# Three later scans of a linear-attention kernel: both decay factors from one VectorE product, their signed copies from ScalarE, and the cap on the inverse length moved

## The chip, the cores and the metric

The kernel runs on one core of one Trainium2 chip. The metric is the device time of one execution in microseconds (us). A core has TensorE (PE, with its weight loads shown as PEld), VectorE (DVE), ScalarE (ACT), GpSimd (POOL) and SyncE (SP), which issues the DMAs here.

## The reference, cut to what matters

Four batches, eight heads, 768 tokens, 48 features a head. A complex decay, clipped in length, drives a linear attention; what comes out goes through a Fourier mixer with an MLP, then a token MLP and a second channel MLP.

```python
mag = np.sqrt(a_re * a_re + a_im * a_im)
scale = np.minimum(mag, 0.999) / (mag + 1e-06)
ar, ai = a_re * scale, a_im * scale            # the normalized factor
for t in range(S):
    S_re, S_im = ar*S_re - ai*S_im + k v, ar*S_im + ai*S_re
    y[t] = q[t] @ S_re
x -> x + real(fft(fft(x))) -> norm -> MLP -> token MLP -> MLP
```

## The kernel before, in words

Each batch has a **chain** (the functions `scan`, the chunk part of `stage1`, and `stage2`, the mixer) and a **dense** part (`mlp`, `tok1`, `tok2`, `mlp2`). The dense part of batch b-1 is emitted beside the chain of batch b. The chain of batch 0 has a scan of its own (`first_scan`), which this change touches only in where its small tile `both` is allocated; `scan` runs for batches 1, 2 and 3 and is called the first, second and third later scan here.

A later scan holds 64 chunk halves on two sets of 64 partitions and walks through 49 steps of cumulative products. Sixteen tiles have three steps each and the seventeenth has one. For each tile `st_b` to `st_d` compute the length of the decay; `st_e` makes the factor tile `A`; `st_f` does the steps on VectorE in PSUM (L623, L624, L625); `st_g` multiplies queries and keys by the running product (L634, L635, L637); `st_t` transposes them on TensorE (L650).

`A` has five planes of 48 features a step: plane 0 the real factor, plane 1 its copy, plane 2 the squared inverse factor, plane 4 the imaginary factor times a per-partition sign `sgn` (-1 on the lower 64 partitions, +1 on the upper), plane 3 the negative of plane 4. The common scaling is `c1` (written by VectorE, L595). Plane 0 is a GpSimd product (L597), plane 4 a VectorE product with the sign (L599), planes 1, 2 and 3 come from ScalarE (L598, L600, L601). Plane 2 drives a third running product, the squared inverse length. At the second step of each tile (`j == CL`, CL is 1) VectorE takes the minimum of that product and `R_CAP` in place (L620); there are 48 of these in the three scans.

In program order the factors of tile i+1 are made after step two of tile i (`part2(i + 1)` in the loop at the end of `scan`). `A` has two buffers; `raw`, the loaded decays, share a tag of ten buffers (`"e"`).

The order on each engine's queue is found at build time by a scheduler that goes by priorities and a time estimate of its own; on VectorE, ScalarE and GpSimd the dense stream comes first, then the weight conversions, then the chain; on TensorE the chain comes first. Engines execute their queues in that order. During the first later scan the kernel also converts 64-bit-packed weights into two-part fp32 weights (`convert`: ScalarE L191, L192, L205; VectorE L194, L199; GpSimd L196, L206; a DMA in, L185, and one out, L207).

Of the kernel before, what the change touches and what calls it, by code (L numbers as in the profile page):

```python
# [8 lines left out]
F32 = mybir.dt.float32  # L9
# [3 lines left out]
ACTF = mybir.ActivationFunctionType  # L13
ALU = mybir.AluOpType
# [9 lines left out]
NT = 3  # L24
# [5 lines left out]
CF = (2, 2, 2, 2, 2, 0, 8, 0)  # L30
AN = (5, 6, 6, None)
WC = (0, 0, 0, 0, 0, 0, 10, 12)
WZ, CL = 0, 1
XL = (0,), (0, 1, 2, 3, 4, 5)
AH = 4
KS, EN = 5, 3
# [1 line left out]
XP = [((0, 96), (96, 96), (192, 96), (288, 96))] + [((0, 288), (288, 96))] * 4  # L38
NR = [((0, 192),)] * 5
KT, PF, PD = (0, 1), ((2, 0), (2, 1)), (((1, 0), (1, 1)), ((1, 1),))  # L40
O = (0, 1, 0)
HOLD = mybir.DependencyInfo(mybir.DependencyClass.NoSync, mybir.DependencyReason.SCHED_ONLY)
CHK_A, CHK_E = 6.0e4, 1.0e-7
CHK_B, CHK_C, R_CAP = 1.5e-9, 1.0e18, 1.0e24
# [4 lines left out]
def with_ap(ap, offset, dims):  # L49
    return bass.AP(ap.tensor, ap.offset + offset, [list(ap.ap[0])] + [list(d) for d in dims])  # L50
# [3 lines left out]
def attn_fft_mixer_kernel(ctx: ExitStack, tc: tile.TileContext, aL, xL, vL, wL, qN, kN, vN, arN, aiN,  # L54
# [37 lines left out]
    def alloc(tag, shape, dt=F32, name=None):  # L92
        n = 1
        for x in shape[1:]:
            n *= x
        t = pool.tile([128, SIZE[tag]], dt, tag=tag, bufs=BUFS[tag], name=name or tag)
        return shaped(t[0:shape[0], 0:n], shape)
# [21 lines left out]
    sgn = misc[:, 224:225]  # L119
# [14 lines left out]
        ge.memset(gm[j], 0.0)  # L134
    xT = pool.tile([112, 4, S], F32, name="xT")
    chk = pool.tile([128, 3], F32, name="chk")
    low = pool.tile([128, len(SL4)], F32, name="low")
    lnc = pool.tile([128, 5], F32, name="lnc")
    tiny, shift, top, eps, wee = (lnc[:, j:j + 1] for j in range(5))
# [174 lines left out]
    def first_scan(t, knd, qk):  # L314
# [7 lines left out]
        big = {}  # L322
        last = [None]
        away = []
        both = pool.tile([128, 2], F32, name="both")

        def vq(x):

# [219 lines left out]
    def scan(b, t, knd, qk):  # L548
# [40 lines left out]
        def st_e(i):  # L589
            d = t[i]  # L590
            n, raw, tm = d["n"], d["raw"], d["tm"]
            x, r, tt, c1 = (tm[:, j, :].rearrange("p (a c) -> p a c", c=48) for j in range(4))
            A = alloc("A", [128, 4, 240], name="A")
            A = with_ap(A, 0, [(240, n), (48, 5), (1, 48)])
            ve.scalar_tensor_tensor(out=c1, in0=r, scalar=-2.0 / ACL, in1=tt, op0=ALU.max, op1=ALU.mult)  # L595
            ve.scalar_tensor_tensor(out=x, in0=r, scalar=-2.0 / ACL, in1=x, op0=ALU.min, op1=ALU.mult)
            ge.tensor_tensor(out=A[:, :, 0, :], in0=raw[:, :, 0, :], in1=c1, op=ALU.mult)  # L597
            se.copy(out=A[:, :, 1, :], in_=A[:, :, 0, :])  # L598
            (ge if O[2] else ve).scalar_tensor_tensor(out=A[:, :, 4, :], in0=raw[:, :, 1, :], scalar=sgn, in1=c1, op0=ALU.mult, op1=ALU.mult)  # L599
            se.activation(out=A[:, :, 2, :], in_=x, func=ACTF.Square)  # L600
            se.activation(out=A[:, :, 3, :], in_=A[:, :, 4, :], func=ACTF.Copy, scale=-1.0)  # L601
            d["A"] = A
            P = palloc("p", [128, NT, 144])
            d["P"] = P[:, 0:n, :].rearrange("p n (c f) -> p n c f", c=3)

        def st_f(i, j):
            d = t[i]
            P, A = d["P"], d["A"]
            s = d["s0"] + j
            if s == 0:  # L610
                se.copy(out=P[64:128, 0, 0, :], in_=A[64:128, 0, 0, :])
                se.copy(out=P[64:128, 0, 1, :], in_=A[64:128, 0, 4, :])
                se.copy(out=P[64:128, 0, 2, :], in_=A[64:128, 0, 2, :])
                ve.memset(P[0:64, 0, 0, :], 1.0)
                ve.memset(P[0:64, 0, 1, :], 0.0)
                ve.memset(P[0:64, 0, 2, :], 1.0)
                return
            prev = P[:, j - 1] if j else t[i - 1]["P"][:, t[i - 1]["n"] - 1]
            if j == CL:
                ve.tensor_scalar(out=prev[:, 2, :], in0=prev[:, 2, :], scalar1=R_CAP, scalar2=None, op0=ALU.min)  # L620
            cur = P[:, j]
            y = ytmp[s % 2]
            ve.tensor_tensor(out=cur, in0=prev, in1=A[:, j, 0:3, :], op=ALU.mult)  # L623
            ve.tensor_tensor(out=y, in0=prev[:, 1::-1, :], in1=A[:, j, 3:5, :], op=ALU.mult)  # L624
            ve.tensor_tensor(out=cur[:, 0:2, :], in0=cur[:, 0:2, :], in1=y, op=ALU.add)  # L625

        def st_g(i):
            d = t[i]
            m, P, xx, s0 = d["m"], d["P"], d["xx"], d["s0"]
            y1, y2 = ybuf[0][i % 2], ybuf[1][i % 2]  # L630
            x1 = xx[:, :, 0, :].unsqueeze(2).to_broadcast([128, m, 2, 48])
            o1 = with_ap(y1, 0, [(128, m), (64, 2), (1, 48)])
            o2 = with_ap(y2, 0, [(128, m), (64, 2), (1, 48)])
            ve.tensor_tensor(out=o1, in0=x1, in1=P[:, 0:m, 0:2, :], op=ALU.mult)  # L634
            ve.tensor_tensor(out=xx[:, :, 1, :], in0=xx[:, :, 1, :], in1=P[:, 0:m, 2, :], op=ALU.mult)  # L635
            x2 = xx[:, :, 1, :].unsqueeze(2).to_broadcast([128, m, 2, 48])
            ve.tensor_tensor(out=o2, in0=x2, in1=P[:, 0:m, 0:2, :], op=ALU.mult)  # L637
            sp.dma_start(out=knd[0, :, s0:s0 + m, :], in_=y1[0:64, 0:m, :])
            sp.dma_start(out=knd[1, :, s0:s0 + m, :], in_=y2[64:128, 0:m, :])
# [721 lines left out]
```

## Time and profile before

| | |
|---|---|
| median of 3 runs | 1092.18 us (1091.67 to 1096.09) |
| profiled execution: its time / its span | 1093.5 us / 1091.7 us |
| TensorE busy | 978.8 us (90%) |
| VectorE busy | 769.3 us (70%) |
| ScalarE busy | 511.1 us (47%) |
| GpSimd busy | 417.9 us (38%) |
| mean granted TensorE clock | 0.966 |

The span runs from the first to the last instruction. Busy time merges overlapping instructions of one engine. An instruction's duration includes its pipeline's fill and drain, so neighbours on VectorE or ScalarE can overlap a little. The share of an engine over the whole span is an average over stages with different limits.

### The profile page before, as it was taken

The page shows a single profiled execution, that of the slowest core. Times are in us where ns is not written, and L with a number is a line of the kernel's source. Part 1 is how long each engine was busy: PE and PEld are TensorE (multiplying, and loading weights), DVE is VectorE, ACT ScalarE, POOL GpSimd, SP SyncE. Part 2 cuts the span into 40 slices and gives each one's busy share as a digit, 9 for nine tenths or more (in the row PEclk, how much of TensorE's full clock was granted, in tenths as well). Part 3 has the DMA queues.
Part 4 walks back from the last instruction along what each step waited for, and adds up shares of the span by engine and source line. Part 5 has one row for each costly group of instructions (what it writes and reads, how often), then busy time and mean ns, then how long its engine had stood idle before and what let it go on. Part 6 is the DMA issues. An engine that isn't in the chain of part 4 may idle for free.

```text
span 1091.7 us, 21067 instructions
## 1 busy us (share of the span) xinstructions
PE 978.8 (90%) x7314; PEld 915.3 (84%) x7314; DVE 769.3 (70%) x2083; ACT 511.1 (47%) x1425; POOL 417.9 (38%) x541
## 2 busy tenths in 40 slices
PE   1567788999899988999998999999897999999997
PEld 0337766989788986899997899999787999999997
DVE  6988887999999678999658879974734433433332
ACT  6753446777875236877216556842224112121111
POOL 6625994673676454345336312424512002000000
PEclk9988896999999999899999999999998999999999
DMA  6238943776668563465575345665303434543432
GB/s 219 48 101 233 290 165 118 252 264 206 200 235 270 162 180 113 117 184 175 156 198 148 100 139 187 203 165 132 128 17 117 146 114 135 159 156 127 163 101 76
DMA packets 101537, 174.66 MB, mean 160 GB/s; under 512 B 11056, under 2 KB 61104, under 8 KB 100912
## 3 DMA queue, kind: packets, MB, share of 16 engines
q1 hardware_dynamic: 101424, 173.24, 51.5%
q8 instruction: 60, 0.98, 0.4%
q14 instruction: 53, 0.43, 0.1%
HBM read 133.88 MB, written 39.32 MB: 159 GB/s over the span
## 4 chain that ended last, share of the span: by engine, by line
PE 68%; DVE 16%; DMA 6%; POOL 4%; ACT 3%; issue 2%; SPq 0%; POOLq 0%; DVEq 0%; ACTq 0%
PE l L956 24%; PE l L934 23%; PE s L761 4%; DMA cvt<-wL 3%; PE s L650 2%; PE s L1047 2%; PE s L810 2%; DVE cvt L199 2%; DVE ws L1002 2%; PE s L1036 1%; PE s L816 1%; PE s L1161 1%; POOL cvt L196 1%; DVE ws L996 1%; PE s L1179 1%
## 5 line engine op out<-in xcount | busy, mean ns | idle before, releaser
L956 PE MATMUL l<-w,h 128*128 128x384 f32 x1728 | 326.5, 339 | 6.8 <-DVE h L947 4.0
L934 PE MATMUL l<-th,w 128*128 128x384 f32 x1152 | 316.0, 344 | 8.8 <-DVE h L947 4.3
L956 PEld LDWEIGHTS l<-w,h 128*128 128x128 f32 x1728 | 297.2, 188 | 11.1 <-DVE h L947 6.3
L934 PEld LDWEIGHTS l<-th,w 128*128 128x128 f32 x1152 | 213.1, 191 | 12.2 <-DVE h L947 6.1
L934 PE MATMUL l<-tl,w 128*128 128x384 f32 x576 | 196.3, 341 | 3.6 <-DVE tl L918 3.6
L938 ACT ACTIVATE h<-l 128x384 fp32r<-128x384 f32 x192 | 94.1, 490 | 213.2 <-PE l L934 212.7
L959 DVE TENSOR_TENSOR u<-u,l 128x384 f32<-128x384 f32 x192 | 105.3, 549 | 83.1 <-PE l L956 82.4
L947 DVE SCALAR_TENSOR_TENSOR h<-l,h 128x384 fp32r<-128x384 f32 x160 | 88.5, 553 | 91.0 <-ACT h L938 90.8
L934 PEld LDWEIGHTS l<-tl,w 128*128 128x128 f32 x576 | 110.3, 191 | 4.2 <-DVE tl L918 4.2
L196 POOL TENSOR_TENSOR cvt<-cvt 128x384 int32<-128x384 int32 x56 | 66.3, 1190 | 38.3 <-DVE cvt L194 7.3
L761 PE MATMUL s<-qkt 112*96 112x96 f32 x512 | 57.8, 263 | 11.0 <-DVE sc L768 11.0
L472 PE MATMUL s<-misc,y 128*112 128x128 f32 x96 | 22.2, 379 | 47.3 <-DVE y L450 44.5
L761 PEld LDWEIGHTS s<-qkt 112*96 112x96 f32 x512 | 51.8, 173 | 13.8 <-DVE sc L768 12.0
L472 PEld LDWEIGHTS s<-misc,y 128*112 128x112 f32 x96 | 14.8, 183 | 57.0 <-POOL tm L366 19.1
L1146 POOL TENSOR_TENSOR xl<-u,xh 128x384 fp32r<-128x384 f32 x18 | 17.9, 1005 | 107.1 <-ACT xh L1145 107.1
L206 POOL TENSOR_TENSOR w<-cvt,w 128x384 fp32r<-128x384 f32 x44 | 52.2, 1197 | 8.3 <-ACT w L205 8.0
L199 DVE SCALAR_TENSOR_TENSOR cvt<-cvt 128x384 int32<-128x384 int32 x56 | 45.9, 828 | 5.9 <-POOL cvt L196 5.8
L579 POOL TENSOR_TENSOR tm<-tm 128x144 f32<-128x144 f32 (+1 forms) x51 | 26.8, 526 | 58.9 <-ACT tm L578 58.6
L945 POOL TENSOR_TENSOR h<-full,h 128x384 fp32r<-128x384 f32 x32 | 33.8, 1057 | 37.2 <-ACT full L944 35.4
L623 DVE TENSOR_TENSOR p<-p,A 128x144 f32<-128x144 f32 x144 | 44.6, 310 | 2.1
L650 PE MATMUL s<-misc,y 128*112 128x128 f32 x288 | 45.2, 276 | 0.9 <-DVE y L634 0.3
L794 POOL TENSOR_TENSOR yc<-Aa,gm 48x384 f32<-48x384 f32 x18 | 21.0, 1164 | 62.4 <-DVE Aa L787 62.4
(232 smaller groups left out, 1940.8 us busy)
## 6 DMA issues: line engine op xcount, KB each, us to landing
w<-wscr SPq DMA_DIRECT2D x180, 384.0 KB, 3.4
cvt<-wL SPq DMA_DIRECT2D x56, 384.0 KB, 5.0
wscr<-w SPq DMA_DIRECT2D x44, 384.0 KB, 3.7
Kn<-kn SPq DMA_DIRECT2D x64, 192.0 KB, 3.7
kn<-y SPq DMA_DIRECT2D x96, 96.0 KB, 2.6
raw<-aL SPq DMA_DIRECT2D x48, 144.0 KB, 3.1
xx<-xL SPq DMA_DIRECT2D x48, 144.0 KB, 2.9
V<-vL SPq DMA_DIRECT2D x32, 144.0 KB, 3.2
```

What stands on the lines that cost most here:

```text
L196: x = ge.tensor_tensor(out=a, in0=a, in1=lo, op=ALU.add)
L199: rest(ve.scalar_tensor_tensor(out=a, in0=hi, scalar=-0x80000000, in1=a, op0=ALU.bitwise_and, op1=ALU.bitwise_or))
L206: ge.tensor_tensor(out=parts[:, 1, :], in0=a.bitcast(F32), in1=r32(parts[:, 0, :]), op=ALU.subtract)
L472: te.transpose(ps[:, j, :], y[:, j, 0:112], ident)
L623: ve.tensor_tensor(out=cur, in0=prev, in1=A[:, j, 0:3, :], op=ALU.mult)
L650: te.transpose(ps[:, j, :], y[:, j, 0:112], ident)
L761: te.matmul(out=ps[:, j, :], lhsT=K[:, hc, :], rhs=Q[:, hc, :])
L934: te.matmul(out=ps, lhsT=w1[:, wi, kt * 128:kt * 128 + 128], rhs=x[g][:, kt, :], start=(n == 0), stop=(n == 8))
L938: x = se.activation(out=hi, in_=ps, func=ACTF.Relu)
L947: ve.scalar_tensor_tensor(out=lo, in0=ps, scalar=0.0, in1=r32(hi), op0=ALU.max, op1=ALU.subtract)
L956: te.matmul(out=ps, lhsT=hs[m][:, hi, tt * 128:tt * 128 + 128], rhs=w2[:, wi, :], start=(n == 0), stop=(n == 8))
L959: ve.tensor_tensor(out=u[tt], in0=u[tt], in1=ps, op=ALU.add)
```

## The change

`st_e` of the later scans makes a tile `A` with six planes. One VectorE product multiplies both halves of `raw` by `c1` and writes planes 0 and 5. ScalarE makes planes 3 and 4 from plane 5 by a copy with a per-partition scale: the columns of `both`, which hold -`sgn` and +`sgn`. GpSimd has no part in `st_e` any more. The cap in the running product goes away; the product of the inverse length with the keys in `st_g` takes the minimum with `R_CAP` as it reads. The tile `both` is allocated at the start, so that the later scans can use it.

```diff
-            A = alloc("A", [128, 4, 240], name="A")
-            A = with_ap(A, 0, [(240, n), (48, 5), (1, 48)])
+            A = alloc("A", [128, NT, 288], name="A")
+            A = with_ap(A, 0, [(288, n), (48, 6), (1, 48)])
             ve.scalar_tensor_tensor(out=c1, in0=r, scalar=-2.0 / ACL, in1=tt, op0=ALU.max, op1=ALU.mult)
             ve.scalar_tensor_tensor(out=x, in0=r, scalar=-2.0 / ACL, in1=x, op0=ALU.min, op1=ALU.mult)
-            ge.tensor_tensor(out=A[:, :, 0, :], in0=raw[:, :, 0, :], in1=c1, op=ALU.mult)
+            ve.tensor_tensor(out=A[:, :, 0:6:5, :], in0=raw, in1=c1.unsqueeze(2).to_broadcast([128, n, 2, 48]), op=ALU.mult)
+            for j in range(2):
+                se.activation(out=A[:, :, 3 + j, :], in_=A[:, :, 5, :], func=ACTF.Copy, scale=both[:, j:j + 1])
             se.copy(out=A[:, :, 1, :], in_=A[:, :, 0, :])
-            (ge if O[2] else ve).scalar_tensor_tensor(out=A[:, :, 4, :], in0=raw[:, :, 1, :], scalar=sgn, in1=c1, op0=ALU.mult, op1=ALU.mult)
             se.activation(out=A[:, :, 2, :], in_=x, func=ACTF.Square)
-            se.activation(out=A[:, :, 3, :], in_=A[:, :, 4, :], func=ACTF.Copy, scale=-1.0)
...
-            if j == CL:
-                ve.tensor_scalar(out=prev[:, 2, :], in0=prev[:, 2, :], scalar1=R_CAP, scalar2=None, op0=ALU.min)
...
-            ve.tensor_tensor(out=xx[:, :, 1, :], in0=xx[:, :, 1, :], in1=P[:, 0:m, 2, :], op=ALU.mult)
+            ve.scalar_tensor_tensor(out=xx[:, :, 1, :], in0=P[:, 0:m, 2, :], scalar=R_CAP, in1=xx[:, :, 1, :], op0=ALU.min, op1=ALU.mult)
```

## Rows read from the trace of the kernel before

**Rows 1.** The page: busy us, share of the span, instructions of each engine.

```profile
PE 978.8 (90%) x7314; PEld 915.3 (84%) x7314; DVE 769.3 (70%) x2083; ACT 511.1 (47%) x1425; POOL 417.9 (38%) x541
```

**Rows 2.** Windows: stretch, length, busy PE, PEld, DVE, ACT, POOL, clock, DMA share, GB/s.

```profile
185.00:345.00 160.00, 149.42 (x877) 141.03 (x876) 152.79 (x441) 122.17 (x345) 98.21 (x126) 1.00 0.69 227
345.00:397.00 52.00, 50.71 (x707) 47.45 (x707) 33.41 (x72) 13.79 (x31) 21.51 (x21) 1.00 0.67 188
397.00:446.00 49.00, 37.50 (x222) 30.92 (x219) 43.39 (x128) 29.88 (x94) 23.68 (x33) 0.87 0.41 126
446.00:580.00 134.00, 133.89 (x1228) 128.49 (x1226) 106.38 (x322) 74.58 (x224) 57.06 (x82) 0.99 0.60 172
...
600.00:725.00 125.00, 125.00 (x767) 120.35 (x766) 108.99 (x376) 80.01 (x246) 37.36 (x73) 1.00 0.52 157
...
780.00:840.00 60.00, 49.50 (x289) 43.98 (x288) 32.67 (x73) 22.33 (x58) 19.69 (x21) 0.91 0.23 73
```

**Rows 3.** Waits of PE, 185 to 345 us: total us, times, longest.

```profile
PE l L934 <- DVE h L947: 4.3, 6, 1.8
PE l L1179 <- ACT R L1167: 1.7, 1, 1.7
```

**Rows 4.** Groups on DVE, 185 to 345 us: busy us, mean ns | idle before.

```profile
L947 DVE SCALAR_TENSOR_TENSOR h<-l,h 128x384 fp32r<-128x384 f32 x38 | 20.9, 550 | 2.8 <-ACT h L938 2.8
L959 DVE TENSOR_TENSOR u<-u,l 128x384 f32<-128x384 f32 x36 | 19.5, 542 | 0.0
...
L599 DVE SCALAR_TENSOR_TENSOR A<-raw,misc,tm 128x144 f32<-128x144 f32 x16 | 9.3, 582 | 0.0
L596 DVE SCALAR_TENSOR_TENSOR tm<-tm 128x144 f32<-128x144 f32 x16 | 7.5, 467 | 0.0
L634 DVE TENSOR_TENSOR y<-xx,p 128x288 f32<-128x288 f32 x16 | 7.2, 448 | 0.2
...
L585 DVE SCALAR_TENSOR_TENSOR tm<-tm 128x144 f32<-128x144 f32 x14 | 6.4, 459 | 0.1
L595 DVE SCALAR_TENSOR_TENSOR tm<-tm 128x144 f32<-128x144 f32 x16 | 5.2, 327 | 0.0
...
L620 DVE TENSOR_SCALAR p<-p 128x48 f32<-128x48 f32 x16 | 3.3, 206 | 0.1
```

**Rows 5.** Groups on ACT, 185 to 345 us (lnc is a per-partition operand).

```profile
L575 ACT ACTIVATE tm<-tm,lnc 128x144 f32<-128x144 f32 x14 | 5.9, 422 | 2.2 <-POOL tm L569 2.2
...
L601 ACT ACTIVATE A<-A 128x144 f32<-128x144 f32 x16 | 5.1, 318 | 2.6 <-DVE A L599 2.5
L598 ACT COPY A<-A 128x144 f32<-128x144 f32 x16 | 5.0, 309 | 3.6 <-POOL A L597 3.5
```

**Rows 6.** Groups on POOL, 185 to 345 us.

```profile
L597 POOL TENSOR_TENSOR A<-raw,tm 128x144 f32<-128x144 f32 x16 | 8.5, 528 | 10.8 <-DVE tm L595 10.7
```

**Rows 7.** Timeline of DVE: start us, length us, line, operation.

```profile
301.23 0.29 DVE L595 SCALAR_TENSOR_TENSOR tm<-tm 128x144 f32<-128x144 f32 x1
...
302.13 1.10 DVE L599 SCALAR_TENSOR_TENSOR A<-raw,misc,tm 128x144 f32<-128x144 f32 x1
303.15 1.37 DVE L199 SCALAR_TENSOR_TENSOR cvt<-cvt 128x384 int32<-128x384 int32 x1
...
309.50 0.30 DVE L623 TENSOR_TENSOR p<-p,A 128x144 f32<-128x144 f32 x1
```

**Rows 8.** Timeline of POOL over the same stretch.

```profile
301.60 0.49 POOL L597 TENSOR_TENSOR A<-raw,tm 128x144 f32<-128x144 f32 x1 [1.04 <-DVE tm L595]
302.06 2.04 POOL L206 TENSOR_TENSOR w<-cvt,w 128x384 fp32r<-128x384 f32 x2
```

**Rows 9.** Timeline of ACT over the same stretch.

```profile
303.26 0.33 ACT L601 ACTIVATE A<-A 128x144 f32<-128x144 f32 x1 [0.59 <-DVE A L599]
```

**Rows 10.** Waits of SP's queue, 185 to 345 us.

```profile
SPq L207 <- POOL w L206: 30.9, 20, 7.6
```

**Rows 11.** Groups on DVE, 596 to 725 us (the third later scan).

```profile
L599 DVE SCALAR_TENSOR_TENSOR A<-raw,misc,tm 128x144 f32<-128x144 f32 x16 | 7.1, 442 | 0.0
...
L585 DVE SCALAR_TENSOR_TENSOR tm<-tm 128x144 f32<-128x144 f32 x14 | 4.2, 301 | 1.0 <-POOL tm L579 0.7
```

More of the change, by code (lines that the diff above doesn't have):

```diff
@@ L32 @@
 WC = (0, 0, 0, 0, 0, 0, 10, 12)
-WZ, CL = 0, 1
+WZ = 0
 XL = (0,), (0, 1, 2, 3, 4, 5)
@@ L40 @@
 KT, PF, PD = (0, 1), ((2, 0), (2, 1)), (((1, 0), (1, 1)), ((1, 1),))
-O = (0, 1, 0)
 HOLD = mybir.DependencyInfo(mybir.DependencyClass.NoSync, mybir.DependencyReason.SCHED_ONLY)
@@ L136, in attn_fft_mixer_kernel @@
     chk = pool.tile([128, 3], F32, name="chk")
+    both = pool.tile([128, 2], F32, name="both")
     low = pool.tile([128, len(SL4)], F32, name="low")
@@ L324, in first_scan @@
         away = []
-        both = pool.tile([128, 2], F32, name="both")
         def vq(x):
```

## The prediction

> **What bounds the kernel now.** I read the page first: TensorE is busy 90% of the span, no other engine over 70% [rows 1]. So the question for any change off TensorE is where TensorE stands idle, and the table of stretches answers it [rows 2]. In the second and third later scan (446 to 580 and 600 to 725 us) TensorE is busy 133.9 of 134 and 125.0 of 125 us: VectorE time saved there can buy nothing directly. In the first later scan (185 to 345 us) it is different: VectorE is busy 152.8 of 160 us and TensorE 149.4, so 10.6 us of TensorE are empty and VectorE is the fuller engine. The waits of that stretch name VectorE: the largest is TensorE waiting for the low half of the hidden layer, L947, 4.3 us in 6 waits [rows 3]. Then comes a stretch set by the mixer, 397 to 446 us, with 11.5 us of TensorE idle, and a like one from 780 to 840 us with 10.5 us [rows 2]; both end a chain, so a chain that arrives earlier leaves more dense work to fill them. I count on the first later scan, and only partly on the rest.
>
> **Removed from VectorE.** L599, 16 times 582 ns, 9.3 us, and the seventeenth tile of one step, which I take at 0.3 us here and for the new product, between the 206 ns of L620 (48 features) and the 0.29 us of 144: 9.6 us in the first later scan. L620, 16 times 206 ns: 3.3 us [rows 4]. Together 12.9 us.
>
> L599 is dearer than its size. A three-step operation of the same form took 0.29 us when nothing was in its way (L595 at 301.23 us), while L599 at 302.13 us took 1.10 us [rows 7]; GpSimd was on its own factor product L597 from 301.60 to 302.09 and on conversions until 304.10 us [rows 8]. The VectorE operation ended as the first conversion did, and the next, L199, lasted 1.37 us up to about the end of the second. So VectorE operations on two operands in SBUF are held while GpSimd is at work. The Trainium skill, "GPSIMD Engine Reference", section Specifications, says that GpSimd shares its SBUF interfaces with VectorE and contends with its instructions of two SBUF inputs; by that rule, which these rows bear out, taking L597 away helps, but the new product, with two SBUF inputs as well, stays exposed to the conversions.
>
> **Added to VectorE.** The product of both factors, 128x288 from two SBUF operands, has no row of this size and form. Lower bound: 448 ns, L634 at 128x288 with one operand in PSUM [rows 4]. What stalls add is read from neighbours that have no GpSimd twin: L585 has 459 ns, so 459 - 290 = 169 ns of stall; L595 has 327, so 37 ns; the old L599, twin included, has 582 - 290 = 292 ns. The three give 485, 617 and 740 ns. I take 617, since L585 meets the conversions and nothing of its own: 16 x 0.617 + 0.3 for the short tile = 10.2 us; the ends are 8.1 and 12.1 us. [...]
>
> L596 runs beside L597 now (467 ns) and would fall to L585's 459 at the least and to L595's 327 at best: 0.1 to 2.2 us saved. I take 0.1. The capped product with the keys becomes a three-operand form; L947 (three-operand, 550 ns) against L959 (two-operand, 542 ns), both 128x384 with one operand in PSUM, prices that at 8 ns, 0.1 us in 16.
>
> **VectorE's sum in the first later scan.** -12.9 + 10.2 - 0.1 + 0.1 = -2.7 us. Bounds: with everything at the cheap end -12.9 + 8.1 - 2.2 + 0.1 = -6.9 us; with the stalls kept -12.9 + 12.1 + 0.1 = -0.7 us. In the third scan the stalls are smaller (L599 442, L585 301 ns [rows 11]): -7.1 - 0.3 - 3.3 + 16 x (0.448 + 0.011) + 0.3 = -3.1 us, with L620 and the short tile as above,, but TensorE is full there, so the chain arrives some 3 us earlier at the mixer stretch of 780 to 840 us. I allow 1 us for that, with 0 and 3 as its ends: TensorE's order there is fixed and may keep its holes.
>
> **GpSimd.** L597 goes: 8.5 us of work and 10.8 us in which GpSimd's queue stood at it waiting for L595 [rows 6]. The conversions queue behind it, and SP's write-back behind them (30.9 us at L207 [rows 10]). I cost this at nothing in the sum: TensorE waited mostly for VectorE, hardly for weights [rows 3]. It is the first rival.
>
> **ScalarE.** One negation (318 ns) is replaced by two passes with a per-partition scale. The scale operand's price is not shown in the scan; L575 has a per-partition bias and 422 ns [rows 5]. The bounds are 318 and 422; I take 422, the form that is nearest. That is 16 x (2 x 0.422 - 0.318) + about 0.4 for the short tile = 8.8 us more in the first later scan, 122.2 to 131.0 of 160 us. It is covered: L601 ended at 303.59 us [rows 9], and the first step that reads that tile began at 309.50 us [rows 7], 5.9 us later. The product's 617 ns stand against the 582 and 528 ns of L599 and L597, so its planes come about 0.1 us later, and the passes take 2 x 0.422 - 0.318 = 0.5 us more; 0.6 fits in 5.9. What queues behind a pass that waits for the product is the dense activation L938 and then L947; ScalarE already waits there for L599 and L597, 2.5 + 3.5 us [rows 5], and after the change only for the product. If the cover failed, all 8.8 us would be on the path.
>
> No DMA is added or moved; `raw` is read by one instruction in place of two, so its buffer comes free no later.
>
> **Sum.** -2.7 - 1.0 = -3.7, say -4 us. Against the profiled execution: span 1091.7 to 1087.7, its own time 1093.5 to 1089.5 us. The median shown, 1092.18, stands 1.3 below that execution's time; so the forecast median is 1088 us. For this case alone the bounds give 0.7 to 10, and I expect 1 to 7 us: 1085 to 1091.
>
> **The rivals.**
>
> Rival 1, GpSimd sets the pace of the first later scan: the conversions move up by the 19 us of queue that L597 held, VectorE loses most stalls (its -6.9), and the 10.6 us of TensorE idle in that stretch close. Time 1092.2 - 10.6 = 1081.6 us. For it: SP's wait of 30.9 us at L207, and the 1.10 and 1.37 us stalls. Against it: little of TensorE's waiting there is for weights.
>
> Rival 2, nothing arrives: the time saved on VectorE is spent by waiting elsewhere and TensorE, with the same work in a fixed order, ends within 2 us of before: 1092 us. For it: TensorE is full in two of three scans, and the free price of the product, 448 ns, is about that of the two operations it replaces, 290 + 206 ns.
>
> Rival 3, slower: ScalarE's queue. A signed pass at the queue's head waits for a product that a GpSimd conversion holds for up to 1 us; behind it stands L938, then L947, then TensorE. If the 8.8 us added in the first later scan reach L947, the time is about 1101 us. It decides once VectorE's wait for L938, 2.8 us now [rows 4], grows by more than the 4 us gained. Against it: 6.0 us of waiting at L598 and L601 are given up in exchange. The Trainium skill, "ScalarE: Activation LUTs", section Rules for kernel authors, would put a multiplication on VectorE, not ScalarE; by that rule this rival is right, and the trace agrees so far that each pass costs 318 to 422 ns.
>
> **How the numbers follow.** Chances: forecast 0.38, rival 1 0.24, rival 2 0.16, rival 3 0.22. A measurement of this kernel tells about 0.5%, 5.5 us, from no change. Faster than 1086.7 us: rival 1 and a third of the forecast, 0.36. Slower than 1097.6: most of rival 3, 0.18. Within: 0.46. The range takes in rival 1 with 2.6 us to spare and stops short of rival 3's centre: 1079 to 1099 us.
>
> **What would show it.** In the profile after: the product at 128x288 near 0.5 to 0.65 us in the first later scan and near 0.46 in the third; L596 not above 467 ns; two passes of about 0.42 us on ScalarE; no group for L597, L599 and L620; VectorE's busy time in the first later scan down by about 3 us and TensorE's idle time in it below 10.6 us; still full TensorE in the other two. The forecast is wrong if the first later scan is not shorter, if VectorE waits longer for L938, or if the holes of the two mixer stretches change by more than the scan does, since the scheduler orders every queue anew.

## The result: slower by 0.8%, where a gain of 4 us was forecast

| | before | after |
|---|---|---|
| median, six runs each | 1095.09 us (1091.67 to 1096.71) | 1102.38 us (1098.93 to 1104.79) |
| after / before, 95% interval | | 1.0080 [1.0053, 1.0106] |
| profiled execution: time / span | 1093.5 / 1091.7 us | 1099.99 / 1098.2 us |
| mean granted TensorE clock | 0.966 | 0.957 |

The forecast was 1088 us with a range of 1079 to 1099; the third rival's 1101 us is what came. The two medians stand 7.3 us apart; in six runs the kernel before stands 2.9 us above the three-run median that the forecast started from.

The page of the changed kernel, busy time by engine, answers to [rows 1]:

```profile
PE 985.9 (90%) x7314; PEld 921.0 (84%) x7314; DVE 763.9 (70%) x2035; ACT 524.9 (48%) x1476; POOL 392.9 (36%) x490
```

VectorE has 5 us less to do, GpSimd 25 us less, ScalarE 14 us more. TensorE, with the same matmuls, is busy 7.1 us longer; its idle time hardly moved (112.9 to 112.3 us): here the lost time shows as matmuls at the lower mean clock. Of the 7.1 us, 2.5 lie ahead of 185 us, where the scans in question have not begun and both kernels had done the same work (971 for 972 matmuls in 118.73 for 116.25 us). The table of stretches, columns as in [rows 2]:

```profile
185.00:345.00 160.00, 147.93 (x861) 139.43 (x860) 150.16 (x422) 124.82 (x358) 88.96 (x108) 0.99 0.68 222
345.00:397.00 52.00, 50.41 (x670) 46.70 (x670) 34.67 (x74) 14.65 (x33) 22.50 (x22) 1.00 0.64 185
397.00:446.00 49.00, 38.80 (x263) 32.58 (x260) 40.20 (x118) 29.59 (x89) 19.43 (x25) 0.88 0.49 146
446.00:580.00 134.00, 133.62 (x1188) 127.79 (x1188) 104.57 (x313) 78.08 (x240) 51.18 (x72) 0.98 0.59 166
...
600.00:725.00 125.00, 125.00 (x774) 120.32 (x773) 104.93 (x356) 87.08 (x272) 30.47 (x59) 1.00 0.53 158
...
780.00:840.00 60.00, 47.35 (x290) 42.20 (x287) 35.00 (x71) 21.68 (x57) 23.60 (x22) 0.89 0.23 78
```

In the first later scan VectorE's busy time fell by 2.6 us, near the 2.7 of the forecast, yet TensorE did fewer matmuls in it (861 for 877) and was idle 12.1 us for 10.6. The scan itself became shorter: its steps run from 191.9 to 339.7 us, before from 190.5 to 340.4. What fell behind is the dense stream beside it: ScalarE carried out 36 of the activations L935 (L938 before) in this stretch, 38 before. Where the 6.5 us between the two spans are lost can be read by counting the dense stream's matmuls (those that write the tile l) in both traces and comparing when each began. In medians over 20 us the changed kernel was 0.2 us late at 180 to 200 us, 3.8 at 300 to 320, between 3.7 and 7.5 up to 460, a steady 4.5 to 5.1 from 460 to 820, and 6.6 from there on. So about 4.5 us are lost up to 460 us, most of it beside the first later scan, none in the third scan, and the last 2 us in the mixer stretch of 780 to 840 us. The stretch's rows:

```profile
L935 ACT ACTIVATE h<-l 128x384 fp32r<-128x384 f32 x36 | 17.5, 487 | 0.3 <-PE l L931 0.3
L598 ACT ACTIVATE A<-A,both 128x144 f32<-128x144 f32 (+1 forms) x34 | 12.1, 409 | 0.9 <-DVE A L596 0.8
```

The second row is the signed passes. VectorE's groups of the same stretch, the larger form alone, against [rows 4] (columns as there; L596 is the new product, L595 was L596, L594 makes `c1` and was L595, L632 is the capped product with the keys):

```profile
L596 DVE TENSOR_TENSOR A<-raw,tm 128x288 f32<-128x288 f32 x16 | 8.0, 497 | 0.0
L595 DVE SCALAR_TENSOR_TENSOR tm<-tm 128x144 f32<-128x144 f32 x16 | 7.6, 477 | 0.0
...
L594 DVE SCALAR_TENSOR_TENSOR tm<-tm 128x144 f32<-128x144 f32 x16 | 6.4, 401 | 0.0
...
L632 DVE SCALAR_TENSOR_TENSOR xx<-p,xx 128x144 f32<-128x144 f32 x16 | 4.8, 298 | 0.0
```

The product in the third scan, against [rows 11]:

```profile
L596 DVE TENSOR_TENSOR A<-raw,tm 128x288 f32<-128x288 f32 (+1 forms) x17 | 7.5, 440 | 0.0
```

The waits of the first later scan, against [rows 3, 4] (total, times, longest):

```profile
POOL tm L578 <- ACT tm L577: 16.7, 6, 4.3
POOL tm L568 <- ACT sq L565: 13.6, 8, 3.8
...
PE l L931 <- DVE h L944: 6.2, 6, 3.2
...
DVE h L944 <- ACT h L935: 2.6, 3, 1.9
...
PE s L647 <- ACT tm L577: 1.8, 1, 1.8
```

TensorE waits longer for the low half of the hidden layer (6.2 us for 4.3, the longest 3.2 for 1.8), and GpSimd, rid of its product, stands waiting longer for ScalarE (L565 and L577 are the next tile's length chain). Before, the same two waits were:

```profile
POOL tm L579 <- ACT tm L578: 11.5, 6, 3.3
...
POOL tm L569 <- ACT sq L566: 4.7, 4, 2.3
```

### The profile page after: what moved, and what is told of

It reads as the page before. It is cut to its first block, busy times and chain, and to the rows that moved or that the text cites. A ratio compares the mean times of both kernels' runs of the same rounds, so it can differ in the third digit from the quotient of the medians.

```text
span 1098.2 us, 20956 instructions
## 1 busy us (share of the span) xinstructions
PE 985.9 (90%) x7314; PEld 921.0 (84%) x7314; DVE 763.9 (70%) x2035; ACT 524.9 (48%) x1476; POOL 392.9 (36%) x490
## 4 chain that ended last, share of the span: by engine, by line
PE 62%; DVE 6%; ACT 3%; DMA 2%; issue 1%; POOL 1%; SPq 0%; POOLq 0%; DVEq 0%; ACTq 0%
PE l L953 22%; PE l L931 21%; PE s L758 3%; PE s L1044 2%; PE s L647 2%; PE s L1033 2%; PE s L807 2%; DMA cvt<-wL 2%; PE l L1176 1%; PE s L813 1%; PE s L1158 1%; DVE ws L993 1%; PE s L1176 1%; PE s L773 1%; PE s L911 1%
## 5 line engine op out<-in xcount | busy, mean ns | idle before, releaser
L931 PE MATMUL l<-th,w 128*128 128x384 f32 x1152 | 321.5, 347 | 12.4 <-DVE h L944 7.2
L931 PEld LDWEIGHTS l<-th,w 128*128 128x128 f32 x1152 | 214.3, 192 | 18.3 <-DVE h L944 10.5
L935 ACT ACTIVATE h<-l 128x384 fp32r<-128x384 f32 x192 | 94.5, 494 | 216.1 <-PE l L931 216.1
L471 PEld LDWEIGHTS s<-misc,y 128*112 128x112 f32 x96 | 14.5, 181 | 55.9 <-POOL tm L365 18.9
L568 POOL TENSOR_TENSOR tm<-sq 128x144 f32<-128x144 f32 (+1 forms) x51 | 28.4, 558 | 64.9 <-ACT sq L565 59.4
L620 DVE TENSOR_TENSOR p<-p,A 128x144 f32<-128x144 f32 x144 | 44.4, 308 | 2.5 <-ACT A L599 0.8
```

The lines of the kernel that those rows point to most:

```text
L471: te.transpose(ps[:, j, :], y[:, j, 0:112], ident)
L931: te.matmul(out=ps, lhsT=w1[:, wi, kt * 128:kt * 128 + 128], rhs=x[g][:, kt, :], start=(n == 0), stop=(n == 8))
L935: x = se.activation(out=hi, in_=ps, func=ACTF.Relu)
```

## The experiments

A change of this kernel does two things: it changes the instructions, and the scheduler then orders every queue anew. **Theory 1**: the new order costs the time. **Theory 2**: the operations do. To part them, an order was written into the kernel: each instruction gets a key, and neighbours on a queue are tied.

```python
for a, b in zip(keys, keys[1:]):
    tc.add_manual_dep(REC[tag, b].ins, REC[tag, a].ins.name, HOLD, reason="order")
```

That the ties by themselves cost nothing that can be measured shows below: held kernels came out at 0.9989 to 1.0009 of the kernel before. In kernels so held the trace gives one line (L304 to L308) for every instruction; the names of the tiles tell them apart. Each ratio is to the kernel before on the same chip, in five rounds.

### The new operations in the old order

The product stands at L599's place, the two passes and the copy together at the later of L598's and L601's places (43 of 51 copies moved back for it). ScalarE's queue for one tile:

```diff
-L598 copy, L600 square, L601 negation
+L600 square, s0 signed pass, s1 signed pass, copy
```

> The changed kernel's instructions, with every engine's queue held in the order that it had before the change (the product stands where L599 stood, the two signed passes and the copy where the later of L598 and L601 stood). Theory 1, the order: the slowdown comes from the new order of the queues; then this is no slower than before, 1086 to 1094 us against 1092 to 1095, ratio 0.994 to 1.001. Theory 2, the operations: the signed passes on ScalarE and the longer way to the factors delay the dense work; then this is slow as the changed kernel is, ratio 1.005 to 1.010, 1098 to 1104 us.

Measured: 1100.74 us, ratio 1.0067 [1.0044, 1.0091]. The operations cost the time in the old order too.

### The old operations in the new order

```diff
-keys = the queues of the kernel before
+keys = the queues of the changed kernel
```

> The instructions of before, with every engine's queue in the order of the changed kernel (the cap stands before the step it guards; GpSimd's factor product is left to the scheduler, all else is held). Theory 1, the order: slow as the changed kernel, ratio 1.005 to 1.010. Theory 2, the operations: as before, ratio 0.998 to 1.002.

Measured: 1102.49 us, 1.0083 [1.0060, 1.0107]. An order found for other instructions may fit these badly, so this says that order can matter as much as operations, not that the new one is bad for the new operations. Both theories live.

### One edit alone, each in the scheduler's order

The limit alone (the diff), and the rest of the change without it:

```diff
-            if j == CL:
-                ve.tensor_scalar(out=prev[:, 2, :], in0=prev[:, 2, :], scalar1=R_CAP, scalar2=None, op0=ALU.min)
...
+            ve.scalar_tensor_tensor(out=xx[:, :, 1, :], in0=P[:, 0:m, 2, :], scalar=R_CAP, in1=xx[:, :, 1, :], op0=ALU.min, op1=ALU.mult)
```

> Of the change only the cap: L620 goes, the product with the keys takes the minimum; the scheduler orders the queues anew. Theory 2: 3.3 us of VectorE less in the first later scan, nothing added: ratio 0.996 to 1.000. Theory 1: the new order decides, and the ratio may lie on either side, 0.994 to 1.008.

> Of the change only the product on VectorE and the signed passes on ScalarE; the cap L620 stays in the steps; the scheduler orders the queues anew. Theory 2: the whole loss is here, ratio 1.006 to 1.012. Theory 1: the order decides, ratio anywhere from 0.994 to 1.010.

Measured: the limit 1096.43 us, 1.0026 [1.0010, 1.0042]; the product 1102.72 us, 1.0085 [1.0060, 1.0110]. By these two the loss comes with the product and its passes, but each stands in an order of its own.

### The limit alone in the old order

The first of the two edits above, with every queue tied as in the kernel before.

> The kernel before in its own queue order with only the limit moved: L620 taken out, the limit in the product with the keys. 48 VectorE operations of about 0.2 us, 9.9 us over the three scans, are gone and nothing else stands elsewhere. In the scheduler's own new order this edit cost 2.8 us. If that was the order (theory 1), it is now at 1090 to 1094 us, not slower than before; a saving of VectorE that reached TensorE would show as up to 3 us less. If the three-operand form is what costs (theory 2), it stays at 1096 us.

Measured: 1094.36 us, 0.9989 [0.9969, 1.0008]. Taking 9.9 us from VectorE buys nothing that can be measured, and the limit's loss above was the newly dealt order.

### ScalarE's load alone, and the product without signs

```diff
             se.activation(out=A[:, :, 3, :], in_=A[:, :, 4, :], func=ACTF.Copy, scale=-1.0)
+            se.activation(out=A[:, :, 5, :], in_=A[:, :, 4, :], func=ACTF.Copy, scale=both[:, 1:2])
```

> The kernel before, every queue held in its own order, with one more ScalarE pass for each tile of the later scans: right behind the negation of L601, a Copy of 128x144 with the per-partition scale into a plane of the factors' tile that nothing reads. This is the added ScalarE load of the change (about 16 x 0.42 = 6.7 us a scan) without the new product, and without a longer way to the factors. If the load of ScalarE costs the time (theory 2a), it is 4 to 8 us slower than before, about 1099 us. If the cost lies in the way to the factors, product first and passes behind it (theory 2b), or in the orders (theory 1), nothing is read later and the time stays within 2 us of before, 1092 to 1096 us.

Measured: 1094.76 us, 1.0009 [0.9991, 1.0028]. The load by itself is free: theory 2a falls in this form.

```diff
-            ve.tensor_tensor(out=A[:, :, 0:6:5, :], in0=raw, in1=c1.unsqueeze(2).to_broadcast([128, n, 2, 48]), op=ALU.mult)
-            for j in range(2):
-                se.activation(out=A[:, :, 3 + j, :], in_=A[:, :, 5, :], func=ACTF.Copy, scale=both[:, j:j + 1])
+            ve.tensor_tensor(out=A[:, :, 0:5:4, :], in0=raw, in1=c1.unsqueeze(2).to_broadcast([128, n, 2, 48]), op=ALU.mult)
+            se.activation(out=A[:, :, 3, :], in_=A[:, :, 4, :], func=ACTF.Copy, scale=-1.0)
```

> The changed kernel's product on VectorE and its limit in the product with the keys, in the queue order of the kernel before, but without the two signed passes: the product writes the first and the fifth plane directly, and one negation with a constant makes the fourth, as in the kernel before. It leaves out the sign of the second factor on half of the partitions; sizes and counts are otherwise as in the changed kernel. ScalarE then has as much to do as before. If ScalarE's added passes cost the time (theory 2a), it is back at 1090 to 1096 us. If the product itself does, longer on VectorE and ahead of all of ScalarE's passes (theory 2b), it stays near the 1101 us of the new operations in the old order.

Measured: 1094.79 us, 1.0002 [0.9985, 1.0019]. The product costs nothing either, though at these places it lasts longer than in the changed kernel's own order:

```profile
L304 DVE TENSOR_TENSOR A<-raw,tm 128x288 f32<-128x288 f32 x16 | 10.2, 635 | 0.0
```

So in the old order it is neither the load nor the product, but passes behind the product. The timeline of the new operations in the old order shows one tile in the second later scan (start, length, engine, line, operation; in brackets the idle time before and what ended it):

```profile
497.82 1.01 POOL L307 TENSOR_TENSOR h<-full,h 128x384 fp32r<-128x384 f32 x1 [0.21 <-ACT full L307]
...
498.05 1.10 DVE L307 TENSOR_TENSOR A<-raw,tm 128x288 f32<-128x288 f32 x1
...
499.19 0.72 ACT L307 ACTIVATE A<-A,both 128x144 f32<-128x144 f32 x2 [0.96 <-DVE A L307]
499.82 0.30 ACT L307 COPY A<-A 128x144 f32<-128x144 f32 x1
500.02 0.48 ACT L307 ACTIVATE h<-l 128x384 fp32r<-128x384 f32 x1
```

and the kernel without signs the same tile:

```profile
494.96 0.32 ACT L304 ACTIVATE A<-A 128x144 f32<-128x144 f32 x1 [0.20 <-DVE A L304]
495.19 0.30 ACT L304 COPY A<-A 128x144 f32<-128x144 f32 x1
495.39 0.48 ACT L304 ACTIVATE h<-l 128x384 fp32r<-128x384 f32 x1
```

With GpSimd on the low half of the hidden layer, the product took 1.10 us; ScalarE's queue stood 0.96 us, and its next dense activation (h<-l) began 0.83 us after that, against 0.43 us without the signs. Only these 0.40 us are the passes' doing: in the trace without signs this tile's product met GpSimd otherwise and took 0.44 us, and the queue stood 0.20 us.

### How long the group holds the queue

**Theory A**: the cost is the time for which passes and copy hold ScalarE's queue once the product is there. **Theory B**: the scan's steps get their factors later. Four edits of the group, in the old order; the queue behind the product:

```diff
 new operations:      s0 (0.41), s1 (0.41), copy (0.30)
+copy first:          copy, s0, s1
+constant scales:     -1 (0.32), +1 (0.32), copy (0.30)
+one pass more:       negation (0.32), unread pass (0.41), copy (0.30)
+factors, then pass:  negation (0.32), copy (0.30), unread pass (0.41)
```

> The new operations in the old queue order, with one exchange: the copy of plane 0 stands ahead of the two signed passes in place of behind them. The first step's reader, which takes planes 0 to 2, can start 0.8 us earlier; the second, which takes planes 3 and 4, starts 0.3 us later, and ScalarE's queue is held as long as before. Theory A (time for which the queue is held): no change, 1098 to 1102 us. Theory B (factors late): up to some 2 us less, 1096 to 1100 us, if it is the first reader that comes late, else no change.

> The new operations in the old queue order, with both passes scaled by a constant, -1 and 1, in place of the per-partition scale. It leaves out the sign on half of the partitions. A pass of this form took 0.32 us in the negation, against 0.41 us for the scaled form, so each tile's group behind the product is 0.93 us long in place of 1.12 us: the number of passes stays, the price of the scale operand goes. If the second pass is what costs, nearly all of the loss stays, 1098 to 1101 us; if the loss goes by the group's length, with 0.62 us costing nothing and 1.12 us 6 us, about 60% of it stays, 1097 to 1099 us; if the operand is what costs, 1093 to 1096 us.

> The kernel without signs (product on VectorE, one negation, the old queue order), with one more ScalarE pass of the scaled form right behind the negation, into a plane that nothing reads. ScalarE's queue now holds what it holds in the new operations at the same places, a wait for the product and then 0.32 + 0.41 + 0.30 us, but the factors that the scan reads are complete one pass earlier. It leaves out the sign on half of the partitions. If the cost of the signed passes is the time for which they hold ScalarE's queue once the product is there, L938 and L947 behind them (theory A), it is slow as the new operations are, 1098 to 1102 us. If it is that the scan's steps get their factors later (theory B), it stays with the kernel without signs, 1093 to 1096 us.

> The kernel without signs with the same extra pass as in the run with one pass more, but behind the copy in place of ahead of it: the negation and the copy, which the scan reads, stand at the same places as in the kernel without signs, and the pass that nothing reads is last. It leaves out the sign on half of the partitions. ScalarE's queue is held for 1.03 us behind the product as before. If the length of the hold costs the time, it is slow like its twin, 1099 to 1103 us. If the twin was slow because its copy, which the scan reads, came 0.41 us later, it is back at 1093 to 1096 us.

| group behind the product | sum of its durations, us | median, us | ratio, 95% |
|---|---|---|---|
| without signs | 0.62 | 1094.79 | 1.0002 [0.9985, 1.0019] |
| the kernel before, one pass more | 0.73, behind L599 | 1094.76 | 1.0009 [0.9991, 1.0028] |
| constant scales | 0.94 | 1098.10 | 1.0022 [1.0005, 1.0039] |
| one pass more, ahead of the copy | 1.03 | 1102.25 | 1.0057 [1.0036, 1.0078] |
| factors, then pass | 1.03 | 1102.08 | 1.0065 [1.0040, 1.0091] |
| new operations | 1.12 | 1100.74 | 1.0067 [1.0044, 1.0091] |
| copy first | 1.12 | 1101.70 | 1.0060 [1.0038, 1.0082] |

Neighbours on ScalarE overlap, so from the start of its first to the end of its last instruction a group takes less than this sum: 0.52, 0.74, 0.84 and 0.92 us in the median for 0.62, 0.94, 1.03 and 1.12. The loss grows with the length up to 1.03 us; between 1.03 and 1.12 us the intervals show no difference. The last pass that nothing reads costs as much as any: theory B falls. With the new operations the first VectorE step of a tile began a median of 6.6, 3.9 and 4.8 us (first, second, third scan; 51 tiles) after the tile's last factor, 0.1 us at the least, and in the traces of these kernels no such step is recorded waiting for a factor. Only where a scan starts, VectorE waits for three small ScalarE copies (p) that put the first tile's factors into the running product. They stand on the same queue.

One thing besides the queue is in these medians. The traced executions with one pass more ahead of the copy, with the copy first and with the group later (below) took 1106.65, 1107.35 and 1107.11 us, and in each the clock fell at the end of the first mixer stretch (last section). Against the same matmul of the kernel before, TensorE fell back by 7.2 to 7.3 us there within 10 us; the other held traces have no such step. How often it happens in the runs without a trace isn't known, so a part of these kernels' ratios may be the clock.

### The signs in the first later scan only

```diff
+            if b == 1:
+                (two signed passes)
+            else:
+                (one negation)
```

> The new operations in the old queue order, with the two signed passes in the first later scan only; the second and the third take one negation, as in the kernel without signs, and leave the sign out. The prediction put the whole risk into the first later scan, where VectorE is full, and held the second and third, where TensorE is, for insensitive. If that is right, it is as slow as with signs everywhere, 1098 to 1102 us. In the traces of the new operations in the old order, 2 us of 4.5 were lost ahead of 440 us and the rest from 440 to 510 us, in the second scan: by that it lies between, 1095 to 1099 us.

Measured: 1098.24 us, 1.0023 [1.0008, 1.0039], a third of the loss for a third of the tiles. So the first scan isn't alone. The traces say where else: all held kernels have their matmuls in one order, so the lag of each behind the same matmul of the kernel before can be read. With the new operations it was -2.4 us at 185 us, 0.6 at 345, 0.9 at 397, 2.4 at 446, 4.5 at 520, and still 4.5 at 780; without signs 0.6, 0.6, 0.8, 1.0, 1.1 and 1.0. In that trace the second scan loses, from the mixer stretch in which it starts to 520 us; the third loses nothing.

### What stands behind the group

```diff
 the new operations:  s0, s1, copy, (up to three others), L938
+group later:         (up to three others), L938, s0, s1, copy
+group apart:         s0, (up to three others), L938, s1, copy
```

> The changed kernel's operations, all of them, in the old queue order, except that 20 of the 51 groups (two signed passes and the copy) stand behind the dense activation L938 that followed within four places on ScalarE's queue, in place of ahead of it. If the loss comes over L938 and L947, which wait while a group holds the queue (theory A), most of the 6 to 7 us are back: 1093 to 1097 us. If the hold costs through what else stands behind it (the weights' conversions, the evictions of the transposes, the scan's own next tile), it stays at 1099 to 1102 us.

> The same 20 groups, taken apart: the first signed pass stays where it waits for the product, L938 comes next, and the second pass and the copy follow behind L938. L938 then waits for the product and for one pass of 0.41 us, less than in the kernel without signs (0.62 us, which cost nothing). Theory A: 1093 to 1097 us, as with the whole group later or 1 us above it. If it is other work behind the group: 1099 to 1102 us.

Measured: 1106.19 us, 1.0090 [1.0063, 1.0118], and 1100.37 us, 1.0066 [1.0041, 1.0091]. Nothing came back: L938 alone isn't the way. (The group apart shows it better, since the trace of the group later has the fall of the clock.) **Theory C**: VectorE, whose queue is in order too, waits for ScalarE at two places, L947 for L938, and L585 (tm) for the next tile's length chain, and group later may only have exchanged one for the other. Moving the group behind both:

```diff
 the new operations:  s0, s1, copy, L938, L575, L576, L577, L578
+group last:          L938, L575, L576, L577, L578, s0, s1, copy
```

> The changed kernel's operations, all of them, in the old queue order, except that 41 of the 51 groups (two signed passes and the copy) stand up to 12 places later on ScalarE's queue, 9 in the median, as far as the scan's first reader of the tile leaves 2 us in the trace of the new operations. They then stand behind the next tile's length chain (L566, L575 to L578) and behind 39 dense activations L938, and the product has long come when they reach the queue's head. In the traces so far no step of a scan ever waited for its factors, and VectorE's waits for L938 and, at L585, for L579, which itself needs L578, grew together from 10.3 us (before) and 14.5 us (no signs) to 19 to 21 us (the slow kernels). If these two waits are how the held queue costs time (theory C), they fall back to 10 to 14 us and the time to 1092 to 1097 us. If the cost is the ScalarE work itself, wherever it stands in the queue, it stays at 1099 to 1103 us.

> The kernel before, with the same done to its own negation L601 and copy L598: 43 of 51 stand up to 12 places later on ScalarE's queue. ScalarE waited 5.2 us at L601 and 8.1 us at L598 from 185 to 730 us, and those waits go. Theory C: VectorE's waits for L938 and at L585 cannot fall much, 10.3 us now, so that it gains little, 1090 to 1094 us; if the queue's waits at these two cost time before the change as well, up to 5 us less, 1088 us.

Measured: group last 1097.63 us, 1.0032 [1.0015, 1.0048]; its control on the kernel before 1096.19 us, 1.0021 [1.0007, 1.0035], slower, where either reading had it no slower. Half of the loss is back with every operation kept; time and waits lie just above what theory C forecast (1092 to 1097 us, 10 to 14 us). VectorE's waits from 185 to 730 us (total, times, longest), among them the one for the copies p at a scan's start, in turn for the kernel before, without signs, factors then pass, the new operations, group later, and group last:

```profile
DVE h L947 <- ACT h L938: 8.4, 19, 1.1
...
DVE p L614 <- ACT p L613: 3.0, 2, 1.7
...
DVE tm L585 <- POOL tm L579: 1.9, 3, 0.8
```
```profile
DVE h L304 <- ACT h L304: 10.0, 20, 1.4
DVE tm L304 <- POOL tm L304: 4.5, 8, 1.0
DVE p L304 <- ACT p L304: 3.5, 2, 1.9
```
```profile
DVE h L307 <- ACT h L307: 12.4, 23, 2.0
...
DVE tm L307 <- POOL tm L307: 6.2, 9, 1.3
DVE p L307 <- ACT p L307: 4.8, 2, 2.5
```
```profile
DVE h L307 <- ACT h L307: 12.9, 22, 2.2
...
DVE tm L307 <- POOL tm L307: 7.3, 11, 1.4
DVE p L307 <- ACT p L307: 4.8, 2, 2.7
```
```profile
DVE h L308 <- ACT h L308: 10.8, 18, 1.3
...
DVE tm L308 <- POOL tm L308: 8.7, 12, 1.4
...
DVE p L308 <- ACT p L308: 4.9, 3, 2.4
```
```profile
DVE h L308 <- ACT h L308: 9.5, 17, 1.4
DVE tm L308 <- POOL tm L308: 7.0, 9, 1.4
...
DVE p L308 <- ACT p L308: 3.2, 2, 1.9
```

The sums of theory C's two waits are 10.3, 14.5, 18.6, 20.2, 19.5 and 16.5 us, the ratios 1, 1.0002, 1.0065, 1.0067, 1.0090 and 1.0032. The first 4 us of waiting more cost nothing: VectorE, without signs, is also busy 6.1 us less from 185 to 725 us than before (457.2 for 463.3). Group later cut the wait for L938 and grew the other. But the limit alone in the old order has 16.0 us and cost nothing (0.9989), and constant scales have 18.4 us and cost a third of what 18.6 us cost. With the wait for the copies p added the sums rank the kernels held in the old order better: up to 19.1 us (the limit alone; without signs 18.0, one pass more on the kernel before 15.1) no loss that can be measured; 19.7, 20.2 and 22.8 us (group last, signs in one scan, constant scales) 0.2 to 0.3%; 23.4 to 26.0 us (the rest) 0.6 to 0.9%. Only the control on the kernel before, 11.9 us and 1.0021, falls out. The third wait was taken in after the runs, from one trace of each, so theory C is supported for the old order, not settled.

### Other orders

```diff
-            for j in range(2):
-                se.activation(out=A[:, :, 3 + j, :], in_=A[:, :, 5, :], func=ACTF.Copy, scale=both[:, j:j + 1])
+            ge.tensor_tensor(out=A[:, :, 3:5, :], in0=with_ap(A[:, 0, 5, :], 0, [(288, n), (0, 2), (1, 48)]),
+                             in1=with_ap(both, 0, [(0, n), (1, 2), (0, 48)]), op=ALU.mult)
```

> The changed kernel in the scheduler's own order, but with the two signed planes made by one GpSimd product of 128x288 with the two signs, in place of two ScalarE passes. If ScalarE's added load costs the time and the order little (theory 2a), it falls from 1102 to 1091 to 1096 us. If any new order costs what this one does (theory 1), it stays at 1098 to 1104 us. GpSimd gets some 16 x 0.9 us a scan in place of the 16 x 0.53 of L597, and holds VectorE's two-operand instructions meanwhile: a time above 1104 us would be that.

> The kernel without signs (product on VectorE, the limit in the product with the keys, one negation; the sign is left out on half of the partitions) in the order that the scheduler deals for it, in place of the old order in which it took as long as the kernel before. What is above the kernel before is the price of a newly dealt order alone. The limit alone cost 2.8 us in a new order and nothing in the old one; if that is what a new order costs, 1096 to 1099 us. If the order has no price, 1093 to 1096 us; if the changed kernel's own order is bad by itself (the old operations took 9 us more in it), 1100 us or more.

Measured, both in the order the scheduler dealt: the signs on GpSimd 1097.26 us, 1.0025 [1.0009, 1.0042]; without signs 1099.48 us, 1.0055 [1.0034, 1.0076], where the old order gave 1.0002. Two edits that are free in the old order, the limit alone and the product without signs, so cost 0.26 and 0.55% in newly dealt ones; the signs on GpSimd, which came out between their two forecasts, were not tried in the old order. In the changed kernel this and the passes don't add up (0.80% in all, against 0.67% for the passes in the old order); how much of its loss is order stays open.

Nor does the changed kernel, in its own order, show the waits of theory C. VectorE's three waits from 185 to 730 us:

```profile
DVE h L944 <- ACT h L935: 9.0, 13, 2.5
...
DVE p L613 <- ACT p L612: 3.3, 1, 3.3
...
DVE tm L584 <- POOL tm L578: 2.4, 5, 0.8
```

That is 14.7 us, against 13.3 before and 25.0 with the new operations in the old order. ScalarE's waits for the factor products in the same stretch, in turn before (two products), with the new operations in the old order, and in the changed kernel:

```profile
ACT A L598 <- POOL A L597: 8.1, 20, 0.7
...
ACT A L601 <- DVE A L599: 5.2, 12, 0.7
```
```profile
ACT A L307 <- DVE A L307: 15.7, 21, 1.8
```
```profile
ACT A L598 <- DVE A L596: 8.0, 13, 1.5
```

By these waits the scheduler's order has the passes where the product has mostly come. One step of the changed kernel did wait for a factor, 0.8 us (L620 for the copy L599). By which wait the changed kernel loses its 0.8% no run shows.

## Why the prediction was wrong

**The step that failed** is the one that costed ScalarE's added work at nothing: "It is covered: L601 ended at 303.59 us [rows 9], and the first step that reads that tile began at 309.50 us". The cover was real, and it was the cover of the wrong reader. With the old order held, the passes behind the product cost 0.67%, while the product without them cost nothing (1.0002) and no step behind a scan's first waited for a factor: the factors came in time, and what came late was the queue. The same paragraph named what stands behind, "the dense activation L938 and then L947", and weighed against it only the waits given up at L598 and L601. It didn't ask how long the group that follows such a wait holds the queue: 0.32 us for the negation before, 0.52 with the copy, 0.92 us with two signed passes.

**A second term was at nothing without a reason**: the order that the scheduler deals anew. The prediction names it only among its signs of being wrong. Edits that are free in the old order lost 0.26 and 0.55% to it. In the changed kernel's own order VectorE's waits hardly grew and ScalarE waited less for the product than before, so there the queue's way is not shown. Which of the two terms makes the 0.8%, and by which wait, stays open. In the prediction's own sum, the first later scan's -2.7 us and the last mixer stretch's -1 us, both had the wrong sign: by the trace TensorE's dense work lost about 4.5 us up to 460 us and 2 us in the stretch from 780 us.

**The sum for VectorE** had the right sign, and its size agrees by luck: the busy time of the first later scan fell by 2.6 us for 2.7 forecast, but the sum's own terms, from their rows, come to -4.4 us (8.3 us of product for 12.9 removed, 0.2 more in the L596 of before and the capped product). The product took 497 ns in the changed kernel's own order, forecast 617 within 485 to 740; at the old places it took 635. L596 went from 467 to 477 ns, forecast 459; the capped product took 298 ns. Against this stand `c1`'s operation, which the sum left as it was and which took 401 ns for 327, 1.2 us in all, and other dense and conversion work in the stretch than before. The 4.1 us less in 600 to 725 us, for 3.1 forecast, also compare stretches that hold different work. The two passes took 12.1 us for L601's 5.3 (short tile included), 6.8 more, forecast 8.8.

**Where it would be felt**: the first later scan got 2.1 us shorter, and TensorE got nothing, for the dense stream beside it lost more. That VectorE's savings buy nothing where TensorE is full held (the limit alone in the old order: 0.9989). That those scans are therefore indifferent, the silent other half of the argument, held for the third, whose lag stayed the same in the traces of the changed kernel and of the new operations; the second lost at its start in the latter. Of the prediction's three signs of being wrong, two stayed silent: the scan was shorter, and VectorE did not wait longer for L938. The third, a hole of a mixer stretch that changes by more than the scan does, stood at its edge: 12.7 us for 10.5 from 780 to 840 us.

**The rivals.** Rival 3 had the time and, for the old order, the first half of the mechanism: a product beside a GpSimd operation takes 1.10 us, ScalarE's queue stands, the dense activation waits. That its 1101 us came is luck as far as is known: it put 8.8 us of ScalarE work on the path in the first later scan, where the passes took 6.8 and such work by itself cost nothing (1.0009). Its test was wrong, too. VectorE's wait for L938 in the first later scan didn't grow from 2.8 by 4 us; it was 2.6 us in the changed kernel and 5.1 with the new operations in the old order. The ScalarE rule that the prediction set beside it, from the Trainium skill, "ScalarE: Activation LUTs", section Rules for kernel authors (a multiplication belongs on VectorE), came out right for this kernel, but not by the price of a pass: one pass more for each tile cost nothing measurable (1.0009). Rival 1 fell: GpSimd's queue, freed of L597, waited 16.7 and 13.6 us for ScalarE, 11.5 and 4.7 before. Rival 2's reasoning, that savings don't arrive, held for each part that saves, in the old order.

## What to carry to other kernels

Cost a moved operation not only by its reader's slack but by what queues behind it: with the old order held, a group behind a product that can be late cost nothing at 0.62 us of summed durations and 0.6 to 0.7% from 1.03 us on. An engine that is full gains nothing from a faster helper; where it loses is read from when its work begins, not from its busy share. Before a small loss is put on an edit, hold the old queue order and try the edit in it: two edits that were free there cost 0.26 and 0.55% in an order of their own. And an explanation found with the order held has still to be found in the trace of the kernel itself.

## What was not expected of the hardware

A ScalarE copy of 128x144 with a per-partition scale took 409 ns, with a constant 314 to 321 ns.

The profiled execution of the kernel with the copy first took 1107.35 us, above its median of 1101.70. It is one of the three named above. It ran the end of the first mixer stretch at the lower of TensorE's two clocks (1.2 and 2.4 GHz; columns as in [rows 2], the granted clock third from the end):

```profile
420.00:430.00 10.00, 8.40 (x45) 5.82 (x45) 5.48 (x21) 6.00 (x23) 1.29 (x3) 0.73 0.65 206
430.00:440.00 10.00, 10.00 (x33) 7.36 (x33) 3.74 (x15) 4.06 (x13) 2.69 (x6) 0.50 0.09 28
```

The kernel before had 1.00 and 0.69 there; it was busy for all of the first 10 us and for 3.82 us of the second. In the 10 us at 0.50, TensorE was busy throughout with 33 matmuls, after 8.40 busy us of the 10 before. The traces with one pass more and with the group later show 0.66, then 0.50, with TensorE busy for 8.60 and 8.43 us, then throughout. What sets off the fall no run shows. The mean clock of a run doesn't rank the kernels, though: without signs it was 0.958 at a span of 1092.7 us, with the new operations in the old order 0.966 at 1096.2 us.
